# Attention and two MLP layers on one core: the last two blocks of the first layer as one of 512 tokens, 40 masks on ScalarE, tail products in another order

## The chip, the cores and the metric

The kernel runs on one core of a Trainium2 chip. The metric is the device time in microseconds (us) of one execution. The five engines of the core (TensorE, VectorE, ScalarE, GpSimd, SyncE) each take their instructions in the order in which the program lists them; in the rows below they are PE (with PEld for its weight loads), DVE, ACT, POOL and SP. An instruction waits on its engine until what it reads has been written, and everything listed behind it on that engine waits with it.

## The reference

```python
# q, k, v: (4, 8, 576, 64); tau: a scalar; x: 2304 tokens of 512; d_ff: 2048
scores = scale * np.matmul(q, k.transpose(0, 1, 3, 2))
thresh = np.max(scores, axis=-1, keepdims=True) - tau
scores = np.where(scores >= thresh, scores, -1000000000.0)
attn = np.exp(scores - np.max(scores, axis=-1, keepdims=True))
attn = attn / (np.sum(attn, axis=-1, keepdims=True) + 1e-09)
x = ...matmul(attn, v), heads joined...           # (2304, 512)
h = x @ w_in; x = np.maximum(h, 0.0) ** 2 @ w_out            # first layer
h = x @ w_in2; out = h * np.tanh(log1p(exp(h))) @ w_out2     # second layer
```

The weights come as 64-bit floats; the kernel takes them apart with integer operations.

## The kernel before

**Order.** Each piece of work is recorded by `op(opts, fn, r, w, x, due)` or `dma(...)`: the engines that may do it with a planned duration each, the buffers that it reads and writes, and a due time. `Plan.order` then goes forwards and backwards over the recorded pieces, gives each an engine and a place, and emits them in that order. The numbers in `PAR` (due times of the blocks in `blk`, offsets, biases, how many spare buffers each purpose gets) and the planned durations only set that order. So nearly every instruction can change its place when a few of them change.

**Attention.** A pair of heads (`Pair`, 16 of them, 4 per batch entry) has four units of 128 query rows for two heads and one tail unit of the last 64 rows, in which the two heads lie side by side in the 128 partitions. A unit makes scores on PE (`scores`), scales them and takes their row extreme on DVE (`top`, L882), makes the threshold (`most`, L892), takes the exponential on ACT (L908), and on DVE sets what lies under the threshold to zero and sums the row (`mask`, L919). That is 9 masks a pair and 144 in all. Pairs of kind "d" (batch entry 0, and one pair of entry 1) work in float32: PE turns the weights (`turn`, L991), and `turned` or, for the tail, `values` in `values_direct` multiplies with V. The other pairs split the weights into two 16-bit parts, which a DMA turns (`pt`), and `values` in `head` multiplies.

**Tails.** In a tail unit each head has its own 64 columns of the PE array: `pt` is the stationary operand, and the slice `sl` says which half of the columns. Before the change all products of the first head come before those of the second. In `turned` (full units of kind "d") the two heads alternate.

**First layer.** 9 blocks of 256 tokens (`first`, `first_part`); a block's eight parts each make two 128-wide pieces of the hidden layer from x (`mlp_in`, 12 matmuls of 256 columns each, into PSUM buffer `h`), relu and square them on ACT, split them into `gh` and `gl`, and multiply down (`down`, 12 matmuls of 256 columns a piece, into `acc`). A float32 product takes three passes, since both operands are split. Block n needs the attention of all heads for its tokens; block 8 holds the tails of all four entries. Blocks start while attention still runs, and PE takes turns between the two.

**Second layer.** Pairs of blocks as 512 tokens, all its matmuls 512 columns wide (`second`). Its weights (`layer2`) take the places of the first layer's as these come free, and are taken apart by ACT and DVE (`size` L525, `rest` L537, `clamp` L532, `shift` L549, `sign` L555, `to_hi` L583, `to_lo` L594).

**Start.** PE turns the first k and q (`job_direct`, L806), ACT copies them out (L817), then come the first scores. `consts` makes the identity, loads tau and derives from it the scale that `top` uses (L455 to L460). Matmuls of `ones` (`spin`) stand in gaps.

Of the kernel before, what the change touches and what calls it, by code (L numbers as in the profile page):

```python
# [29 lines left out]
    warm=(1, 3, 7),  # L30
    won=("S", "S"),
    land=2.419,
    lag=0.518,
    turns=("h", "s1"),
    kv=(("nat0", "V1"), ("f1", "nat1"), ("KT1", "f0"), ("V0", "KT0")),
    cd=(-150.532, 10.911, -114.568),
    urg=-5.54,
    rawt=23.548,
    kinds="dddd",
    cgen=1.383,  # L40
    split=(),
    ex=dict(cw=1, cr=6, raw=17, pd=2, sc=3),
    exo=("cw", "pd", "sc", "cr", "raw"),
    blk=list((17.026, 77.25, 181.004, 262.558, 368.796, 471.734, 577.967, 790.694, 936.347)),
    tb2=145.883,
    down2=89.229,
    sp=(0, 0),
    off=(170.46, 68.826, 37.695, -205.928, 58.656, 43.101, -191.105, -38.461),
    ahead=(10.872, 128.518, 9.367, -61.853, 3.491, 155.716, -16.749, 483.826, 162.488, -31.72),
    start=-197.714,  # L50
    area=dict(sc=("x0", "x1"), hl=("x2",)),
    jobahead=19.381,
    fbi=6,
    stay=1.0,
    stayt=150.0,
    kinds2="ssss",
    kb=("dhss", "ssss", "ssss"),
)
# [22 lines left out]
class Plan:  # L81
# [6 lines left out]
    BIAS = {"V": 1.26, "A": 0.34, "P": 3.463, "S": 0.46}  # L88
# [239 lines left out]
def attention_moe_moe_kernel(ctx: ExitStack, tc: tile.TileContext, q, k, v, tau, w1i, w1o, w2i, w2o, out):  # L328
# [75 lines left out]
    def rot(*places):  # L404
# [59 lines left out]

# [160 lines left out]
    def pow2(name, raws, junk, due):  # L625
# [24 lines left out]
        op({"T": 0.22}, lambda e: mm(t()[:, 0:n], ones, mx(), True, True), r=[mx, K], w=[t], due=due + 0.1)  # L650
# [123 lines left out]
    def job_direct(p, due):  # L774
# [10 lines left out]
        for x, dst, z, (j0, j1) in todo:  # L785
# [24 lines left out]
            t = op({"T": 0.15 * (j1 - j0)}, turn, r=[raw, K], w=[o], due=due - z)  # L810
# [34 lines left out]
    def unit(p, g, hh, j, due):  # L845
# [24 lines left out]
        op({"T": (1.2 if direct else 0.85) if hh < 2 else 0.65 if direct else 0.48}, scores, r=[QT, KT], w=ss, due=due,  # L870
# [34 lines left out]
    def weigh(p, hh, j, i, sc, m, nt, due):  # L905
        ex = sbuf(place("e", "e0", "e1"), [128, 576], F32)
        op({"A": 0.67},
           lambda e: nc.scalar.activation(  # L908
               out=ex(), in_=sc(), func=AF.Exp, bias=m()[:, i:i + 1], scale=-1.0),
           r=[sc, m], w=[ex], due=due + 1.5 - URG, tab=("exp", "ln"))  # L910
# [5 lines left out]
        l = p.l  # L916

# [10 lines left out]
    def head(p, g, hh, u, ex, due):  # L928
# [35 lines left out]
        op({"T": 0.41 if hh < 2 else 0.9}, values, r=[pt, V], w=[o], due=due + 7 + O_VA, half=1)  # L964
# [3 lines left out]
    def values_direct(p, g, hh, u, ex, last, o, due):  # L968
# [24 lines left out]
        op({"T": 0.6}, turn, r=[ex, K], w=ts, due=due + 2.5 + O_DIR)  # L993
# [38 lines left out]
        op({"T": 1.6}, values, r=[pt, V], w=[o], due=due + 7 + O_VA)  # L1032
        normal(p, g, hh, due)

    def turned(p, j, due):
# [21 lines left out]
        op({"T": 0.14}, lambda e: nc.tensor.transpose(o()[:, 128 * j:128 * j + 128], xt(), ident), r=[xt, K], w=[o], due=due + 1)  # L1057
# [52 lines left out]
    def attention(b, groups, t0, t1, tails):  # L1110
        n = NPR * (4 * len(groups) + tails)
        i = 0
        for pr in range(NPR):
# [4 lines left out]
            p.keep = None  # L1118
# [57 lines left out]
    def x_first(n, due):  # L1176
        xh, xo = sbuf("xh", [128, 2, 4, 128], F32R), sbuf("xo", [128, 2, 4, 128], F32R)
        o = pbuf(rot("s0", "s1"), [128, 1024])
        for t in range(2):
            for g in range(2):  # L1180
# [8 lines left out]
                op({"T": 0.218}, turn, r=[xl, K], w=[o], due=due - 0.5)  # L1189
# [84 lines left out]

    def second():
# [220 lines left out]
```

## Time and profile before

| | |
|---|---|
| median of 3 runs | 1029.93 us (1028.37 to 1031.53) |
| the profiled execution | 1031.52 us, its span 1029.7 us |
| PE busy | 1002.4 us (97%), 8581 matmuls |
| DVE busy | 617.9 us (60%) |
| ACT busy | 622.0 us (60%) |
| PE's share of the chain that ended last | 83% |

The span runs from the first to the last instruction of the profiled execution; its own time is 1.8 us longer. Matmuls overlap in the records, so the time that one costs is read from start to start, not from its own duration.

### The profile page before, as it was taken

What the parts mean: (1) busy time and instruction counts of PE and PEld (TensorE: products, weight loads), DVE (VectorE), ACT (ScalarE), POOL (GpSimd) and SP (SyncE); (2) the same over time, 40 slices, a digit from 0 to 9 for tenths busy, and PEclk for the clock granted to TensorE, in tenths of its full rate; (3) what the DMA queues carried; (4) which work ended last, traced back from release to release, by engine and by line L of the source; (5) the groups of instructions that cost most, each with busy time, mean ns of one, the idle gap of its engine ahead of it and who ended that gap; (6) DMA issues with size and microseconds to landing.
All of it is one profiled execution on the core that took longest, in us unless ns stands there. A gap on an engine that the chain in (4) does not pass through costs nothing.

```text
span 1029.7 us, 21534 instructions
## 1 busy us (share of the span) xinstructions
PE 1002.4 (97%) x8581; PEld 888.2 (86%) x8581; DVE 617.9 (60%) x1442; ACT 622.0 (60%) x1143; POOL 0.8 (0%) x7
## 2 busy tenths in 40 slices
PE   5999999999999999999999999999999999999997
PEld 4666789889888998889999999988888888888897
DVE  5999999998899887989765137971211211211111
ACT  5989999777787877877576459962322332232231
POOL 0000000000000000000000000000000000000000
PEclk9999999999999999999999999999999999999999
DMA  9732247798788988887674123521100110010010
GB/s 286 207 112 86 87 139 146 156 157 174 164 164 150 163 158 172 149 156 137 138 204 149 42 68 108 196 91 30 45 8 1 41 41 1 21 41 1 1 41 21
DMA packets 231188, 109.48 MB, mean 106 GB/s; under 512 B 194608, under 2 KB 212016, under 8 KB 231088
## 3 DMA queue, kind: packets, MB, share of 16 engines
q1 hardware_dynamic: 230816, 107.98, 44.8%
q8 instruction: 67, 1.10, 0.4%
q14 instruction: 33, 0.27, 0.1%
q10 hardware_dynamic: 272, 0.13, 0.0%
HBM read 58.16 MB, written 14.16 MB: 70 GB/s over the span
## 4 chain that ended last, share of the span: by engine, by line
PE 83%; ACT 5%; DMA 5%; DVE 4%; SPq 2%; issue 1%; ACTq 0%; DVEq 0%
PE acc L435 26%; PE s L435 22%; PE h L435 21%; PE small L435 10%; DMA pt<-hl 2%; DMA area<-in_moe_w_in_dram 2%; ACT e L908 1%; SPq L792 1%; DMA f<-in_q_dram 1%; DMA area<-in_moe_w_out_dram 1%; DVE e L919 1%; PE s L1187 1%; PE h L991 0%; PE acc L991 0%; ACT stg L525 0%
## 5 line engine op out<-in xcount | busy, mean ns | idle before, releaser
L435 PE MATMUL acc<-gh,wo 128*128 128x256 f32 x1152 | 215.4, 280 | 0.0
L435 PE MATMUL h<-xh,wi 128*128 128x256 f32 x1152 | 213.2, 279 | 0.8 <-ACT r L1232 0.5
L435 PEld LDWEIGHTS h<-xh,wi 128*128 128x128 f32 x1152 | 182.4, 192 | 4.7 <-issue 1.6
L435 PEld LDWEIGHTS acc<-gh,wo 128*128 128x128 f32 x1152 | 183.0, 192 | 3.8 <-issue 3.0
L435 PE MATMUL h<-xo,wi 128*128 128x256 f32 x576 | 158.4, 275 | 0.0
L435 PE MATMUL acc<-gl,wo 128*128 128x256 f32 x576 | 158.4, 275 | 0.0
L594 DVE TENSOR_TENSOR gl<-r,gh 128x512 fp32r<-128x512 f32 x90 | 62.2, 691 | 157.7 <-ACT gh L583 157.4
L435 PEld LDWEIGHTS acc<-gl,wo 128*128 128x128 f32 x576 | 110.5, 192 | 0.0
L435 PEld LDWEIGHTS h<-xo,wi 128*128 128x128 f32 x576 | 110.5, 192 | 0.0
L435 PE MATMUL s<-KT,area 64*128 64x512 f16 (+7 forms) x840 | 88.3, 333 | 3.9 <-ACT area L817 2.5
L583 ACT ACTIVATE gh<-r 128x512 fp32r<-128x512 f32 x87 | 54.7, 628 | 46.3 <-PE small L435 24.0
L919 DVE SCALAR_TENSOR_TENSOR e<-area,n,e 128x576 f32<-128x576 f32 x93 | 74.9, 815 | 8.9 <-ACT e L908 8.8
L435 PE MATMUL acc<-wo,gh 128*128 128x512 f32 x240 | 79.7, 379 | 0.0
L882 DVE TENSOR_SCALAR_CACHE_REDUCE area<-s,c 128x576 f32<-128x576 f32 x90 | 71.7, 814 | 7.2 <-PE s L435 6.8
L594 DVE TENSOR_TENSOR pt<-area,pt 128x512 fp32r<-128x512 f32 x18 | 12.5, 692 | 102.1 <-ACT pt L583 102.1
L908 ACT ACTIVATE e<-area,m 128x576 f32<-128x576 f32 x93 | 70.0, 765 | 2.7 <-DVE area L948 1.6
L948 DVE TENSOR_TENSOR hl<-e,hl 128x512 f16<-128x512 f32 (+1 forms) x136 | 61.0, 454 | 7.3 <-ACT hl L943 7.2
L1232 ACT ACTIVATE r<-h 128x512 f32<-128x512 f32 x71 | 42.0, 592 | 35.5 <-PE h L435 28.6
L435 PE MATMUL small<-V,pt 128*128 128x64 f16 (+1 forms) x1540 | 58.9, 194 | 2.4 <-DMA pt<-hl 1.7
L435 PEld LDWEIGHTS <-pt 128*128 128x128 f16 (+1 forms) x1540 | 50.4, 101 | 10.1 <-issue 5.9
L943 ACT ACTIVATE hl<-e 128x576 f16<-128x576 f32 x68 | 46.0, 678 | 19.8 <-DVE e L919 10.3
L1282 ACT ACTIVATE r<-s 128x512 f32<-128x512 f32 x17 | 10.2, 601 | 68.4 <-PE s L435 68.4
(306 smaller groups left out, 2050.3 us busy)
## 6 DMA issues: line engine op xcount, KB each, us to landing
area<-in_moe_w_out_dram SPq DMA_DIRECT2D x20, 512.0 KB, 4.1
area<-in_moe_w_in_dram SPq DMA_DIRECT2D x17, 512.0 KB, 3.6
wi<-in_moe_w_in_dram SPq DMA_DIRECT2D x10, 512.0 KB, 4.1
xx<-xdr SPq DMA_DIRECT2D x36, 128.0 KB, 2.6
x2dr<-stg SPq DMA_DIRECT2D x18, 256.0 KB, 3.1
xdr<-xx SPq DMA_DIRECT2D x32, 128.0 KB, 2.2
f<-in_q_dram SPq DMA_DIRECT2D x24, 128.0 KB, 3.1
V<-in_moe_w_out_dram SPq DMA_DIRECT2D x6, 512.0 KB, 4.1
```

What stands on the lines that cost most here:

```text
L435: nc.tensor.matmul(o, l, r, start=start, stop=stop, skip_group_check=True)
L583: nc.scalar.activation(out=o, in_=i, func=AF.Copy)
L594: VEC[e].tensor_tensor(out=part(lo), in0=src(), in1=f32(part(hi)), op=ALU.subtract)
L792: e.dma_start(out=raw()[:, j0:main, h, :], in_=x[h, 0:512, :].rearrange("(p j) d -> p j d", j=4)[:, j0:main, :],)
L882: nc.vector.tensor_scalar(out=sc(), in0=s()[:, 0:576], scalar1=c()[:, 3:4], scalar2=None, op0=ALU.mult, op1=ALU.min, accum_out=m()[:, i:i ...
L908: lambda e: nc.scalar.activation(out=ex(), in_=sc(), func=AF.Exp, bias=m()[:, i:i + 1], scale=-1.0),
L919: nc.vector.scalar_tensor_tensor(out=ex(), in0=sc(), scalar=nt()[:, i:i + 1], in1=ex(), op0=ALU.is_le, op1=ALU.mult, accum_out=l()[:, 0, u ...
L943: nc.scalar.activation(out=hl()[:, 0:576], in_=ex(), func=AF.Copy)
L948: VEC[e].tensor_tensor(out=hl()[:, a:a + n], in0=ex()[:, z:z + n], in1=hl()[:, z:z + n], op=ALU.subtract)
L1187: nc.tensor.transpose(o()[:, z + c:z + c + 128], xl()[:, c:c + 128], ident)
L1232: nc.scalar.activation(out=halves(r()), in_=turned_out(ph()), func=AF.Relu)
L1282: nc.scalar.activation(out=out, in_=in_, func=AF.Mish)
```

## The change

- The last two blocks of the first layer (7 and 8) become one of 512 tokens (`last_two`, `two_part`), with matmuls of 512 columns, two PSUM buffers (`s0`, `s1`) for the hidden pieces, and `acc`, `h` and `small` for the sums.
- In both `values` functions of the tails the two heads alternate.
- 40 of the 144 masks go to ACT: `cut` (an activation with a very steep negative side sends what lies under the threshold to minus infinity) and `exp`, which also sums the row, take the place of the exponential on ACT and the mask on DVE. `pm` gives the number per pair for each batch entry: 16, 12, 4 and 8 in all.
- tau has a load and an operation of its own; identity is made apart from it.
- Turns of kind "d" use `h` alone once `acc` is taken. The buffers of the second layer's weights and x are laid out anew. All numbers of `PAR` that set the order are new.

```diff
-    warm=(1, 3, 7),
+    warm=(1, 3, 6),
-    turns=("h", "s1"),
+    turns=("h",),
+    pm=(4, 3, 1, 2),
...
     def consts(e):
-        make_identity(nc, ident)
-        nc.sync.dma_start(out=tt[:, 3:4], in_=tau.to_broadcast([128, 1]))
...
+        nc.vector.tensor_scalar(out=tt[:, 5:6], in0=tt[:, 1:2], scalar1=-1.0, scalar2=None, op0=ALU.mult)
...
-    op({"S": 0.5}, consts, w=[K], due=-50.0, load=(0.0, 0.7, 0.7))
+    dma(lambda e: e.dma_start(out=tt[:, 3:4], in_=tau.to_broadcast([128, 1])), "tau", w=[KT_], due=-40.0)
+    op({"V": 0.45}, consts, r=[KT_], w=[K], due=-39.0)
...
+        p.n += 1
+        if p.n * PAR["pm"][p.b] % 9 < PAR["pm"][p.b]:
+            def cut(e):
+                nc.scalar.activation(
+                    out=ex(), in_=sc(), func=AF.Prelu, bias=nt()[:, i:i + 1], scale=-1.0, alpha=3e38)
+
+            def exp(e):
+                nc.scalar.activation(
+                    out=ex(), in_=ex(), func=AF.Exp, bias=tt[:, 5:6], accum_out=l()[:, 0, u:u + 1])
...
         def values(e):
-            for h in ((hh,) if hh < 2 else (0, 1)):
-                sl = slice(0, 128) if hh < 2 else slice(64 * h, 64 * h + 64)
-                for i in range(9):
-                    t = 5 * h + (i if i < 5 else i - 5)
-                    mm(o()[sl, 64 * u:64 * u + 64], pt()[:, i, sl], V()[:, t, 0:64], i == 0, i == 8)
-                    if i < 5:
-                        mm(o()[sl, 64 * u:64 * u + 64], pt()[:, i, sl], V()[:, t, 64:128], False, False)
+            for i in range(9):
+                for z in range(0, 128 if i < 5 else 64, 64):
+                    for h in ((hh,) if hh < 2 else (0, 1)):
+                        sl = slice(0, 128) if hh < 2 else slice(64 * h, 64 * h + 64)
+                        t = 5 * h + i % 5
+                        mm(o()[sl, 64 * u:64 * u + 64], pt()[:, i, sl], V()[:, t, z:z + 64],
+                           i == 0 and z == 0, i == 8)
...
         def values(e):
-            for h in (0, 1):
-                sl = slice(64 * h, 64 * h + 64)
-                for i in range(5):
-                    d = slice(0, 128) if i < 4 else slice(64, 128)
+            for i in range(5):
+                d = slice(0, 128) if i < 4 else slice(64, 128)
+                for h in (0, 1):
+                    sl = slice(64 * h, 64 * h + 64)
                     mm(o()[sl, 64 * u:64 * u + 64], pt()[d, i, sl], V()[d, 5 * h + i, :], i == 0, i == 4)
...
+    def two_part(j, x, acc):
+        d = due_p(j)
+        ph = quarter(False)
+        for f in range(2):
+            mlp_in(0, j, f, ph[f], 0, x, d + 0.1 * f, 512)
+        for f in range(2):
...
+            def down(e, j=j, f=f, wo=wo, gh=gh, gl=gl):
+                for dt in range(4):
+                    o = acc[0]()[:, 512 * dt:512 * dt + 512] if dt < 2 else acc[dt - 1]()[:, 0:512]
+                    for i, (l, z) in enumerate(passes(wo, (gh, gl))):
+                        mm(o, l()[:, f, 128 * dt:128 * dt + 128], z().rearrange("p a n b -> p n b a"),
+                           j == 0 and f == 0 and i == 0, j == 7 and f == 1 and i == 2)
...
     def layer2(j):
-        raws = ("raw0", "raw1", "V")
...
+        raws = ("raw0", "raw1", "raw2")
+        order = 8 * "nat0 nat1 pt0 pt1".split()
...
-    for n in range(NB):
+    for n in range(NB - 2):
         at(blk[n], first, n)
+    at(blk[NB - 2], last_two)
```

What this does to the order is shown at three places. The first is SP's queue at the start of the program, where the loads are issued; before:

```order
L500 DMA xh<-in_moe_w_out_dram 128x1024
L792 DMA wo_74<-in_k_dram 128x4x64 x2
L797 DMA wo_74<-in_k_dram 64x2x64
L492 DMA area<-in_moe_w_in_dram 128x2x512
L453 DMA tt<-in_tau_dram 128x1
L792 DMA wo_74<-in_q_dram 128x4x64 x2
L797 DMA wo_74<-in_q_dram 64x2x64
```

and with the change:

```order
L794 DMA wo_75<-in_k_dram 128x4x64 x2
L799 DMA wo_75<-in_k_dram 64x2x64
L794 DMA wi_82<-in_q_dram 128x4x64 x2
L799 DMA wi_82<-in_q_dram 64x2x64
L502 DMA xh<-in_moe_w_out_dram 128x1024
L464 DMA tt<-in_tau_dram 128x1
L502 DMA xo<-in_moe_w_out_dram 128x1024
```

The three loads of k and the three of q now stand first; the first weights (`xh`) went from ahead of them to behind them, and tau from fifth to eighth issue.

The second is ACT's queue at the start; before, up to the first exponentials:

```order
L525 ACTIVATE wo_92<-xh 128x512
L537 ACTIVATE xh<-xh 128x512
L525 ACTIVATE stg<-area 128x512
L583 ACTIVATE wo_112<-wo_92 128x512
L537 ACTIVATE area<-area 128x512
L817 ACTIVATE KT<-s_114 128x576
L583 ACTIVATE wi_136<-stg 128x512
L525 ACTIVATE stg<-area 128x512
L817 ACTIVATE area<-s_127 128x576
```

and with the change, up to the first `cut` (L918) and `exp` (L922):

```order
L819 ACTIVATE KT<-s_91 128x576
L527 ACTIVATE wi_118<-xh 128x512
L819 ACTIVATE area<-s_105 128x576
L539 ACTIVATE xh<-xh 128x512
L527 ACTIVATE wi_118<-xo 128x512
...
L929 ACTIVATE e<-wi_150,m_151 128x576
L918 ACTIVATE e<-wi_150,n_161 128x576
L527 ACTIVATE stg<-area 128x512
L922 ACTIVATE e,l_186<-e,tt 128x576
```

The copies of the turned k and q (L817, now L819) moved from sixth and ninth place to first and third.

The third is PE where blocks 7 and 8 begin; a part of block 8 before (x in `xh` and `xo`; each row one or two matmuls):

```order
L435 MATMUL h<-xh,wi_565 128x256
L435 MATMUL h<-xo,wi_565 128x256
L435 MATMUL h<-xh,wi_565 128x256 x2
L435 MATMUL h<-xo,wi_565 128x256
...
L435 MATMUL acc<-gh_9302,wo_112 128x256
L435 MATMUL acc<-gl_9318,wo_112 128x256
```

and the first part of the joined block (x in `KT`, `V`, `f`, `e`), behind block 6's last products:

```order
L437 MATMUL acc<-gl_8716,wo_2135 128x256
L437 MATMUL acc<-gh_8714,wo_2135 128x256
L437 MATMUL s_8768<-KT,wi_274 128x512
L437 MATMUL s_8768<-V,wi_274 128x512
L437 MATMUL s_8768<-KT,wi_274 128x512 x2
L437 MATMUL s_8768<-V,wi_274 128x512
L437 MATMUL s_8768<-KT,wi_274 128x512
```

The same number of tokens now takes half as many matmuls, each of twice the columns: 384 of 512 for 768 of 256.

## Rows read from the trace of the kernel before

**Rows 1.** Busy time by stage: us, then each engine (instructions), PEclk, DMA share, GB/s.
```profile
0.00:16.00 16.00, 6.33 (x22) 4.58 (x24) 5.66 (x13) 7.40 (x12) 0.84 (x7) 1.00 0.89 278
16.00:120.00 104.00, 96.73 (x831) 68.75 (x828) 100.64 (x259) 93.01 (x198) 0.00 (x0) 0.98 0.49 142
120.00:530.00 410.00, 405.30 (x4839) 365.45 (x4839) 358.09 (x933) 317.77 (x591) 0.00 (x0) 1.00 0.79 156
530.00:656.00 126.00, 125.46 (x1086) 124.03 (x1085) 70.26 (x114) 87.07 (x147) 0.00 (x0) 1.00 0.33 109
```

**Rows 2.** PE's timeline, 640 to 656 us: start, duration, what, [idle before].
```profile
641.27 0.28 PE L435 MATMUL h<-xo,wi 128*128 128x256 f32 x1
...
643.61 0.28 PE L435 MATMUL h<-xo,wi 128*128 128x256 f32 x1
...
653.22 0.38 PE L435 MATMUL s<-f,wi 128*128 128x512 f32 x1
...
655.81 0.38 PE L435 MATMUL s<-f,wi 128*128 128x512 f32 x1
```

**Rows 3.** All 16-bit tail products as one group: xcount, busy, mean ns, idle before.
```profile
L435 PE MATMUL small<-V,pt 128*64 128x64 f16 x308 | 10.7, 197 | 1.6 <-DMA pt<-hl 1.3 <-DVE xx L1067 0.3
```

**Rows 4.** PE's timeline around one 16-bit tail.
```profile
295.43 0.97 PE L435 MATMUL small<-V,pt 128*64 128x64 f16 x28
296.33 0.38 PE L435 MATMUL h<-xh,wi 128*128 128x256 f32 x1
```

**Rows 5.** PE's timeline around one float32 tail.
```profile
48.21 1.80 PE L435 MATMUL small<-V,wo 128*64 128x64 f32 x20
49.94 0.66 PE L991 MATMUL h<-ident,e 128*128 128x128 f32 x4
```

**Rows 6.** PE's timeline in `turned`, whose two heads (`wo`, `wi`) alternate.
```profile
27.24 0.32 PE L435 MATMUL small<-wo,V 128*64 128x128 f32 x1
27.24 0.32 PE L435 MATMUL small<-wi,V 128*64 128x128 f32 x1
27.40 0.27 PE L435 MATMUL small<-wo,V 128*64 128x128 f32 x1
```

**Rows 7.** PE's timeline at the start.
```profile
5.70 1.38 PE L806 MATMUL s<-ident,wo 128*128 128x128 f32 x5 [3.91 <-DMA wo<-in_k_dram]
9.37 1.39 PE L806 MATMUL s<-ident,wo 128*128 128x128 f32 x5 [2.29 <-DMA wo<-in_q_dram]
...
15.24 2.40 PE L435 MATMUL s<-KT,area 64*128 64x512 f32 x8 [2.48 <-ACT area L817]
```

**Rows 8.** SP's timeline at the start: issues.
```profile
0.74 0.40 SPq L500 DMA_DIRECT2D xh<-in_moe_w_out_dram  x1
...
2.60 0.64 SPq L797 DMA_DIRECT2D wo<-in_k_dram  x1
...
3.92 0.47 SPq L453 DMA_DIRECT2D tt<-in_tau_dram  x1
...
5.70 0.63 SPq L797 DMA_DIRECT2D wo<-in_q_dram  x1
```

**Rows 9.** ACT's and DVE's timelines at the start.
```profile
4.38 0.66 ACT L525 ACTIVATE wo<-xh 128x512 f32<-128x512 f32 x1 [2.36 <-DMA xh<-in_moe_w_out_dram]
...
8.51 0.15 DVE L455 TENSOR_SCALAR tt<-tt 128x1 f32<-128x1 f32 x1 [8.51 <-DMA tt<-in_tau_dram]
...
17.67 0.82 DVE L882 TENSOR_SCALAR_CACHE_REDUCE wi<-s,cd 128x576 f32<-128x576 f32 x1 [0.27 <-PE s L435]
```

**Rows 10.** DVE up to block 0's x: its first low part, and busy times till then.
```profile
119.27 0.69 DVE L1204 TENSOR_TENSOR xo<-s,xh 128x512 fp32r<-128x512 f32 x1
...
8.50:119.30 110.80, 100.18 (x836) 71.36 (x837) 105.59 (x270) 97.04 (x205) 0.00 (x0) 0.98 0.53 157
```

**Rows 11.** Mask and exponential as groups: busy, mean ns, idle before.
```profile
L919 DVE SCALAR_TENSOR_TENSOR e<-area,n,e 128x576 f32<-128x576 f32 x93 | 74.9, 815 | 8.9 <-ACT e L908 8.8
L908 ACT ACTIVATE e<-area,m 128x576 f32<-128x576 f32 x93 | 70.0, 765 | 2.7 <-DVE area L948 1.6 <-DVE hl L948 0.6 <-DVE l L936 0.2
```

More of the change, by code (lines that the diff above doesn't have):

```diff
@@ L29 @@
     merge=8,
-    warm=(1, 3, 7),
+    warm=(1, 3, 6),
     won=("S", "S"),
-    land=2.419,
-    lag=0.518,
-    turns=("h", "s1"),
+    land=1.932,
+    lag=0.832,
+    turns=("h",),
     kv=(("nat0", "V1"), ("f1", "nat1"), ("KT1", "f0"), ("V0", "KT0")),
-    cd=(-150.532, 10.911, -114.568),
-    urg=-5.54,
-    rawt=23.548,
+    cd=(-160.029, 12.621, -161.281),
+    urg=-15.443,
+    rawt=22.691,
     kinds="dddd",
-    cgen=1.383,
+    cgen=7.952,
     split=(),
[L42 to L46, printed above, removed]
+    ex=dict(cw=4, cr=2, raw=32, pd=2, sc=5),
+    exo=("cr", "cw", "sc", "pd", "raw"),
+    blk=list((25.72, 84.953, 185.792, 266.428, 370.172, 474.28, 578.7, 808.575, 941.026)),
+    tb2=136.032,
+    down2=92.619,
     sp=(0, 0),
-    off=(170.46, 68.826, 37.695, -205.928, 58.656, 43.101, -191.105, -38.461),
-    ahead=(10.872, 128.518, 9.367, -61.853, 3.491, 155.716, -16.749, 483.826, 162.488, -31.72),
-    start=-197.714,
+    off=(192.543, 61.874, 12.17, -239.53, 56.556, 58.809, -204.681, -78.195),
+    ahead=(21.758, 102.326, 4.716, -50.865, 1.704, 145.102, -26.751, 495.329, 152.712, 63.594),
+    start=-183.005,
     area=dict(sc=("x0", "x1"), hl=("x2",)),
-    jobahead=19.381,
+    jobahead=19.847,
     fbi=6,
-    stay=1.0,
-    stayt=150.0,
+    stay=1.5,
+    stayt=220.0,
     kinds2="ssss",
     kb=("dhss", "ssss", "ssss"),
+    pm=(4, 3, 1, 2),
 )
@@ L906, in weigh @@
         ex = sbuf(place("e", "e0", "e1"), [128, 576], F32)
[L907 to L910, printed above, removed]
         u = 2 * hh + j if hh < 2 else 0
@@ L916, in weigh @@
         l = p.l
+        p.n += 1
[6 more added lines that the diff above has]
+                    out=ex(), in_=ex(), func=AF.Exp, bias=tt[:, 5:6], accum_out=l()[:, 0, u:u + 1])
+            op({"A": 0.67}, cut, r=[sc, nt], w=[ex], due=due + 1.5 - URG, tab=("exp", "ln"))
+            op({"A": 0.76}, exp, r=[K], x=[ex], w=[l], due=due + 1.9 - URG, tab=("exp", "ln"))
+            return u, ex
+        op({"A": 0.67},
+           lambda e: nc.scalar.activation(
+               out=ex(), in_=sc(), func=AF.Exp, bias=m()[:, i:i + 1], scale=-1.0),
+           r=[sc, m], w=[ex], due=due + 1.5 - URG, tab=("exp", "ln"))
         def mask(e):
@@ L1273, in first_part, with xtile, __init__, __call__ @@
                     "x2", r=[st], w=[x2_dr[n][h]], due=due_f(n, 7) + 7)
+    def xtile(z):
+        return plan.buf(
+            z, lambda: sb.tile([128, 2, 2, 2, 128], F32R, name=z, tag=z), over=HALF[z][3] if z in HALF else ()
+        )
+    class Columns:
+        def __init__(self, bufs, k):
+            self.bufs, self.k = bufs, k
+        def __call__(self, c):
+            return self.bufs[c // 2]()[:, 0:self.k, :, c % 2, :].rearrange("p n a b -> p n b a")
+    def due_p(j):
+        return blk[7] + (blk[9] - blk[7]) * j / 8.0
@@ new lines, in last_two, with turn, src, hi @@
+    def last_two():
+        due = due_p(0)
+        hs, os_ = (xtile("KT"), xtile("f")), (xtile("V"), xtile("e"))
+        for t, n in enumerate((7, 8)):
+            assert len(x_dr[n].wr) == (NPR if n < 8 else NPR * B)
+            o = pbuf(rot("s0", "s1"), [128, 1024])
+            for g in range(2):
+                for a in range(2):
+                    xl = sbuf(rot("xl0", "xl1"), [128, 256], F32)
+                    dma(lambda e, xl=xl, n=n, a=a, g=g: e.dma_start(
+                        out=xl(), in_=x_dr[n]()[:, a, 256 * g:256 * g + 256]),
+                        "xl", r=[x_dr[n]], w=[xl], due=due - 4)
+                    def turn(e, o=o, xl=xl, z=512 * a + 256 * g):
+                        for c in (0, 128):
+                            nc.tensor.transpose(o()[:, z + c:z + c + 128], xl()[:, c:c + 128], ident)
+                    op({"T": 0.218}, turn, r=[xl, KI], w=[o], due=due - 0.5)
+                def src(o=o, g=g):
+                    return o().rearrange("p (a c b) -> p a c b", a=2, c=4)[:, :, 2 * g:2 * g + 2, :]
+                def hi(e, src=src, t=t, y=hs[g]):
+                    if e == "A":
+                        nc.scalar.activation(out=y()[:, t], in_=src(), func=AF.Copy)
+                    else:
+                        nc.vector.tensor_copy(out=y()[:, t], in_=src())
+                def lo(e, src=src, t=t, y=hs[g], z=os_[g]):
+                    nc.vector.tensor_tensor(out=z()[:, t], in0=src(), in1=f32(y()[:, t]), op=ALU.subtract)
+                op({"A": 0.52, "V": 0.6}, hi, r=[o], w=[hs[g]], due=due - 0.4 - URG)
+                op({"V": 0.6}, lo, r=[o, hs[g]], w=[os_[g]], due=due - 0.3 - URG)
+        x = Columns(hs, 2), Columns(os_, 2)
+        acc = [pbuf("acc", [128, 1024]), pbuf("h", [128, 512]), plan.buf("o0", lambda: small, over=("o1", "o2"))]
+        for j in range(NJ):
+            at(due_p(j), two_part, j, x, acc)
```

89 lines of the change are left out of this document (60 added, 29 removed).

## The prediction, made blind

> **What bounds the kernel now.** I read the busy times by stage first [rows 1]. PE is busy for 405.3 of 410 us between 120 and 530 us and for 125.5 of 126 in the stage behind; until 16 us it lacks 9.7 us, from 16 to 120 us another 7.3. So from 120 us on the time is the sum of what PE streams, and a microsecond taken from PE there is a microsecond off the end, unless a new wait takes its place. Ahead of 120 us it is another matter: from 8.5 us to block 0's x, DVE is busy for 105.6 of 110.8 us [rows 10], so there DVE sets the pace as much as PE does.
>
> Then I read PE's timeline from start to start, since the durations overlap: what one matmul costs is the distance to the next.
>
> **The sum, part by part.** It is made against the profiled execution (1031.5 us, span 1029.7); the median of the runs shown is 1.6 us lower, and the predicted time is the median less the gain.
>
> *Blocks 7 and 8 as one of 512 tokens.* From 641.27 to 643.61 us PE starts 21 matmuls of 256 columns (three in each 0.33 us): 2.34 / 21 = 0.1114 us each. From 653.22 to 655.81 it starts 12 of 512 columns: 2.59 / 12 = 0.2158 us each [rows 2]. Two blocks have 8 parts x 2 pieces x 24 products x 2 = 768 matmuls of 256, which become 384 of 512. Each pair saves 2 x 0.1114 - 0.2158 = 0.0070 us, so 384 x 0.0070 = 2.7 us. Both figures are measured on the same kind of product, so the bounds are narrow, 2 to 3 us.
>
> The Trainium skill ("TensorE: Matmul & The Clock Gate", Back-to-back issue gap) gives the warm distance between isolated matmuls as N / 2.4 GHz and 2.5 ns more. By it a pair would save 2 x 109.2 - 215.8 = 2.6 ns, an estimate of 1.0 us for the 384, and the predicted time would be 1020.0 us. The row at 512 columns agrees with it (215.8 ns), the one at 256 does not (111.4 ns); the rows decide.
>
> *16-bit tails.* 308 products [rows 3] are 11 tails of 28. One takes 296.33 - 295.43 = 0.90 us [rows 4]. No row shows these with the heads in turn. The nearest is `turned`, which does alternate, with the same column halves: both heads' products start at 27.24, the next pair 0.16 us later [rows 6]. There the second head lies wholly beside the first. So the price is bounded by 0.90 (nothing overlaps) and 0.45 (all does); I take 0.50, near the row, since 14 pairs each have two weight loads and so little streaming to hide them. 11 x 0.40 = 4.4 us, bounds 0 and 5.0. All eleven lie where PE is the bound.
>
> *Float32 tails.* There are five (kind "d" four times in entry 0, once in entry 1). One takes 49.94 - 48.21 = 1.73 us [rows 5]; by the same row of `turned`, between 0.87 and 1.73. I take 0.98, so 0.75 saved. Three of the five lie ahead of block 0, where DVE is late anyway; I count two, 1.5 us (bounds 0 and 4.3 for all five).
>
> *The start.* k's last load is issued at 2.60 us and PE begins to turn it at 5.70, 3.1 us later; q's at 5.70, turned from 9.37, 3.7 us later [rows 7, 8]. In the new order SP issues k's three loads first and q's right behind. An issue takes some 0.67 us with the gap behind it [rows 8], so the last of k starts at 0.74 + 1.4 = 2.1 and the last of q at 4.1 us; PE turns k at 5.2 and q at 7.8 to 9.2 us. Before, ACT's copy of q came only after weights' work that waits for DVE, so the first scores start at 15.24, 4.5 us after q was turned. Now the copy has two operations ahead of it: k's copy, and the first weights, whose load is issued at 4.8 us and so lands at 8.4 (3.64 us, as from 0.74 to 4.38 [rows 8, 9]). The copy runs from 9.2 to 9.9 us, and scores start at 9.9: 5.3 us sooner. tau is issued at 5.2 instead of 3.92 and lands 4.6 us later as before [rows 8, 9], at 9.8, in time for the first reduction on DVE at about 12.3 (17.67 before).
>
> How much of the 5.3 us lasts depends on DVE. Between 8.5 and 119.3 us it was idle for 5.2 us (110.8 less 105.6 [rows 10]). It now begins 1.3 us later (9.8), and although 16 masks leave it in that stretch, the order gives it other pieces for them (9 copies, 7 shifts, one more pair of score reductions): counted by kind and priced at the distances of the trace, it has some 3 us less to do than before up to block 0's x. With that idle time kept, block 0's x comes 3.1 - 1.3 = 1.8 us sooner, with one more unit of scores done by then, which is worth one or two more. I take 3 us; bounds 0 (DVE and ACT give it all back) and 5.3 (all lasts).
>
> *40 masks on ACT.* DVE loses 40 x 0.815 = 32.6 us, ACT gains 40 x 0.765 = 30.6 at least [rows 11]; `cut` and the sum in `exp` are not in this trace, and the exponential over the same 128x576 is the nearest row. From 120 us on both are off the path (DVE 358 and ACT 318 of 410 us [rows 1]), so I price this at nothing. Its cover is that slack; if it is gone, PE waits for turned weights. In the stretch before 120 us ACT has 93 of 104 us and gets some 5 more, which I have charged to the start.
>
> *Second layer's places and the rest.* Its weights used to be taken apart during block 8 and on into the second layer, PE busy throughout that stage [rows 1]; the joined block gives them twice as long from its first part on. No term. PE's waits after 120 us (4.7 us) may shift either way: 0, bounds -3 and +3.
>
> Sum: 2.7 + 4.4 + 1.5 + 3 = 11.6 us. Profiled execution 1019.9; median 1029.9 - 11.6 = **1018.3 us**.
>
> **The rivals.**
>
> *A, the start is given back.* DVE and ACT together have no less to do before block 0, ACT begins its weights 4 us later than at 4.38 [rows 9], and each ACT mask is two instructions in a row on an engine that also copies for PE. For it: DVE's 95% before 119.3 us [rows 10]. Against: first scores are 5.3 us sooner on paper and both engines have idle time. Then only 2.7 + 4.4 + 1.5 = 8.6 us are left: 1021.3 us, or 1022.8 if the float32 tails go with it.
>
> *B, alternating heads gain nothing.* The products are 64 columns wide, not 128 as in `turned`, so weight loads may set the pace, and these may not overlap. Then 2.7 + 3 = 5.7 us: 1024.2 us. Rows 6 speak against it.
>
> The Trainium skill (the same page, Part 3: Packing small matmuls) says that weight loads overlap running matmuls only where the row groups differ; here both heads use the same 128 rows and differ in columns alone. By it the tails keep their price and the time is B's. No row here shows the loads themselves; that two heads start together on the same rows [rows 6] is against it.
>
> *C, slower: the joined block waits for its hidden pieces.* By the order, a part's pieces are used 10.4 us after they are made (one part down and one part up between them, 4 x 2.6 us), and ACT and DVE work them off between the weights of the second layer, in one queue. If a weight operation stands there and waits for its load or its place, each part is late by what is past that cover, eight times. The change then only turns slower past (11.6 + 3.1) / 8 = 1.8 us per part; at 2.5 us it is 1018.3 + 20 = 1038.3 us. Against: from 530 to 656 us the same kinds of work took ACT 87 of 126 us and PE lacked 0.5 [rows 1].
>
> *D, it shows nothing:* A and B together, 2.7 us or 1027.2, which is within what a measurement tells (0.3%, 3.1 us).
>
> **How the numbers follow.** My forecast has 0.55 (its own range 1013 to 1021, from bounds of tails and start), a larger gain (all upper bounds, 2.7 + 5.0 + 4.3 + 5.3 + 3 = 20.3, so down to 1009.6) 0.05, A 0.18, B 0.07, D 0.06, C 0.09. Below 1012 I leave out 0.05, above 1026 D and C, 0.15: range 1012 to 1026. Faster by over 0.3% (below 1026.8): forecast, larger gain, A and B, 0.85. Same 0.06. Slower 0.09, all C and its like.
>
> **What would show it.** First scores at 9.9 us (within 1). 384 matmuls of 512 columns 0.2158 us apart where blocks 7 and 8 were, without a wait of PE. A 16-bit tail of 28 products in 0.50 us, a float32 one in 1.0. Block 0's x about 2 us sooner than 119.3. DVE's busy time lower by 15 to 33 us, ACT's higher by 10 to 30. Waits of PE between 16 and 120 us of 7 to 10 us; over 10 is A. The prediction is wrong if tails keep 0.90 us (B), if PE's waits behind 530 us exceed 3 us (C), or if waits between 120 and 530 us grow past 8 us, which would mean that ACT has become late there.

## The result, and the profile after

The changed kernel takes 1017.88 us (median of 4 runs, 1016.92 to 1018.24), the kernel before 1029.15 us in the same runs: ratio 0.9885, 95% interval 0.9866 to 0.9905. That is 11.3 us less, against 11.6 forecast (1018.3). Timed once more, beside some of the experiments, the ratio was 0.9886 (0.9869 to 0.9902).

Busy times by stage of the changed kernel, as in [rows 1]:

```profile
0.00:16.00 16.00, 10.10 (x40) 7.16 (x41) 4.15 (x13) 6.84 (x11) 0.85 (x7) 0.86 0.72 200
16.00:120.00 104.00, 95.39 (x847) 67.13 (x847) 99.56 (x261) 98.52 (x218) 0.00 (x0) 0.96 0.55 159
120.00:530.00 410.00, 404.13 (x4866) 365.97 (x4865) 344.86 (x888) 328.49 (x626) 0.00 (x0) 1.00 0.80 153
530.00:656.00 126.00, 126.00 (x714) 113.25 (x713) 93.97 (x149) 105.93 (x172) 0.00 (x0) 1.00 0.46 154
```

PE lacks 8.6 us of 104 in the second stage, 5.9 of 410 in the third and nothing in the fourth, where the joined block stands. DVE is busy for 601.0 us in all (617.9 before), ACT for 636.7 (622.0): DVE loses 16.9 us and ACT gains 14.7, about half of what the forecast counted for the masks.

PE's timeline, the places of [rows 7, 5, 4, 2] in turn: start, one float32 tail, one 16-bit tail, one part of the joined block.

```profile
4.39 1.38 PE L808 MATMUL s<-ident,wo 128*128 128x128 f32 x5 [2.09 <-DMA wo<-in_k_dram]
...
6.73 1.38 PE L808 MATMUL s<-ident,wi 128*128 128x128 f32 x5
...
11.72 2.40 PE L437 MATMUL s<-KT,area 64*128 64x512 f32 x8 [2.30 <-ACT area L819]
...
70.31 0.95 PE L437 MATMUL small<-V,wo 128*64 128x64 f32 x20
71.19 0.66 PE L808 MATMUL s<-ident,wi 128*128 128x128 f32 x4
...
193.23 0.63 PE L437 MATMUL small<-V,pt 128*64 128x64 f16 x28
193.79 0.38 PE L437 MATMUL h<-xh,wi 128*128 128x256 f32 x1
...
590.89 0.38 PE L437 MATMUL s<-KT,wi 128*128 128x512 f32 x1
...
596.07 0.38 PE L437 MATMUL acc<-gh,wo 128*128 128x512 f32 x1
```

A float32 tail takes 71.19 - 70.31 = 0.88 us (1.73 before), a 16-bit one 0.56 (0.90 before). Between the last two rows 24 matmuls start, 5.18 / 24 = 0.2158 us each, without a wait.

ACT's and DVE's timelines at the start, and DVE's first low part of block 0's x, as in [rows 9, 10]:

```profile
10.48 0.66 ACT L527 ACTIVATE wi<-xh 128x512 f32<-128x512 f32 x1 [4.02 <-DMA xh<-in_moe_w_out_dram]
11.04 0.64 ACT L819 ACTIVATE area<-s 128x576 f32<-128x576 f32 x1
...
10.89 0.15 DVE L455 TENSOR_SCALAR tt<-tt 128x1 f32<-128x1 f32 x1 [10.89 <-DMA tt<-in_tau_dram]
...
14.25 0.81 DVE L884 TENSOR_SCALAR_CACHE_REDUCE wi<-s,cd 128x576 f32<-128x576 f32 x1
...
117.27 0.69 DVE L1219 TENSOR_TENSOR xo<-s,xh 128x512 fp32r<-128x512 f32 x1
```

ACT stood before the first weights' load until 10.48 us, with q's copy queued behind; so the first scores came at 11.72, not at the 9.9 of the forecast. SP had issued that load at 4.81 us, as forecast, but it took 5.7 us to land, where the prediction had 3.64. Block 0's x comes 2.0 us sooner than in [rows 10].

### The profile page after: what moved, and what is told of

Same layout as the page of the kernel before. It is cut to its first block, busy times and chain, and to the rows that moved or that the text cites. A ratio compares the mean times of both kernels' runs of the same rounds, so it can differ in the third digit from the quotient of the medians.

```text
span 1016.5 us, 20689 instructions
## 1 busy us (share of the span) xinstructions
PE 991.2 (98%) x8195; PEld 866.9 (85%) x8195; DVE 601.0 (59%) x1395; ACT 636.7 (63%) x1194; POOL 0.9 (0%) x7
## 4 chain that ended last, share of the span: by engine, by line
PE 74%; ACT 6%; DVE 4%; DMA 3%; issue 2%; SPq 1%; ACTq 0%; DVEq 0%
PE s L437 24%; PE acc L437 23%; PE h L437 16%; PE small L437 9%; DMA pt<-hl 1%; DMA f<-in_q_dram 1%; ACT e L929 1%; DVE e L934 1%; SPq L716 1%; ACT e L922 1%; PE s L1202 1%; DVE area L884 1%; ACT e L918 1%; DVE hl L963 1%; DMA pt<-area 0%
## 5 line engine op out<-in xcount | busy, mean ns | idle before, releaser
L437 PE MATMUL acc<-gh,wo 128*128 128x256 f32 (+1 forms) x960 | 190.1, 287 | 0.0
L437 PE MATMUL h<-xh,wi 128*128 128x256 f32 x912 | 169.9, 280 | 0.6 <-ACT r L1247 0.5
L437 PEld LDWEIGHTS acc<-gh,wo 128*128 128x128 f32 x960 | 154.7, 192 | 4.5 <-issue 2.5
L437 PEld LDWEIGHTS h<-xh,wi 128*128 128x128 f32 x912 | 144.7, 192 | 4.0 <-issue 1.9
L437 PE MATMUL acc<-gl,wo 128*128 128x256 f32 (+1 forms) x480 | 135.4, 282 | 0.0
L437 PE MATMUL h<-xo,wi 128*128 128x256 f32 x456 | 125.4, 275 | 0.0
L437 PEld LDWEIGHTS acc<-gl,wo 128*128 128x128 f32 x480 | 92.0, 192 | 1.1 <-DVE gl L596 0.2
L437 PEld LDWEIGHTS h<-xo,wi 128*128 128x128 f32 x456 | 87.5, 192 | 0.0
L437 PE MATMUL s<-KT,wi 128*128 128x512 f32 x192 | 64.9, 379 | 0.0
L437 PE MATMUL s<-f,wi 128*128 128x512 f32 x192 | 64.9, 379 | 0.0
```

The source lines that it names most:

```text
L437: nc.tensor.matmul(o, l, r, start=start, stop=stop, skip_group_check=True)
```

## The experiments

Each kernel was timed beside the kernel before; "by the ratio" is the difference of two ratios times 1029 us. One ratio's interval is 1.2 to 2.0 us to either side, and a difference of two has some 2.4, so differences under that are not settled by the times alone. Where two kernels have the same order, the traces tell more: I matched DVE's instructions one to one and took the difference of their starts. Medians of this difference, in us (positive is later), by the place in us in the kernel that stands second in each row:

| | 20-30 | 40-60 | 100-120 | 160-200 | 300-350 | 450-500 | 900-1000 |
|---|---|---|---|---|---|---|---|
| float32 tails back - changed | -0.1 | -1.0 | 1.1 | 2.1 | 2.1 | 1.7 | 2.2 |
| 16-bit tails back - changed | -0.2 | -0.4 | -0.3 | -0.3 | 1.2 | 2.1 | 2.8 |
| 512 split - changed | -0.5 | -1.5 | -1.5 | -1.5 | -1.8 | -2.5 | 0.8 |
| tails alone - before | -0.9 | -1.5 | -2.3 | -2.9 | -5.3 | -7.1 | -6.5 |
| 40 masks back - changed | -0.6 | 3.6 | 10.6 | 12.8 | 14.4 | 15.5 | 15.6 |
| 24 masks back - changed | 0.1 | -0.5 | -0.4 | 2.1 | 4.5 | 5.3 | 5.5 |
| masks alone - before | -0.1 | 1.1 | 5.4 | 6.7 | 8.2 | 7.9 | 7.5 |
| copy sooner - changed | -0.5 | -1.3 | -1.3 | -1.4 | -3.0 | -2.6 | -2.4 |
| loads sooner - changed | -0.9 | -0.4 | -0.4 | -0.3 | -2.0 | -2.6 | -2.6 |
| other beginning - changed | -1.7 | -3.6 | -3.6 | -3.6 | -4.0 | -4.4 | -4.4 |
| the same, products ahead - changed | -0.7 | -1.1 | -1.1 | -1.1 | -1.4 | -1.4 | -0.9 |
| changed, again - changed | -0.5 | -0.9 | -0.9 | -0.9 | -1.2 | -1.5 | -1.1 |

The last row is scatter: two executions of one kernel differ by 0.9 us after the start, where the first ran longer at half clock (last section), and by 0.2 more in the end. So only growth behind 40 us is read off the first rows.

**Float32 tails back.**

```diff
-            for i in range(5):
-                d = slice(0, 128) if i < 4 else slice(64, 128)
-                for h in (0, 1):
-                    sl = slice(64 * h, 64 * h + 64)
+            for h in (0, 1):
+                sl = slice(64 * h, 64 * h + 64)
+                for i in range(5):
+                    d = slice(0, 128) if i < 4 else slice(64, 128)
```

> The changed kernel with only the five float32 tails' products back in the old order (one head after the other); everything else, the order on all engines too, as changed. In the changed kernel such a tail takes 0.878 us, before 1.728, so 0.85 is in question, five times. Theory 1 (PE's own time is the path also ahead of block 0, all five tails count): 4.2 us slower than the changed kernel. Theory 2 (the step on record: DVE is late anyway ahead of block 0, so only two of the five count): 1.7 us slower, with the rest gone from PE's waits between 16 and 120 us. Rival B (alternating heads gain nothing): 0.

Ratio 0.9914 (0.9902 to 0.9927): 3.0 us slower. The difference grows from -1.0 to 2.1, by 3.1 us, in steps of 0.6, 0.9, 0.7 and 0.9 behind the tails at 48, 70, 91 and 120 us; the fifth, at 153 us, shows no step of its own. So the three ahead of block 0's x count as well: theory 1, less what the waits take up.

DVE's waits from 40 to 120 us show why DVE doesn't hide them (engine, tile and line <- what it waited for: us, times, longest). The two longest in the changed kernel:

```profile
DVE xx L1082 <- ACT e L929: 0.9, 1, 0.9
DVE e L934 <- ACT e L929: 0.7, 1, 0.7
```

And with the tails back:

```profile
DVE e L934 <- ACT e L929: 1.6, 2, 0.9
DVE xx L1082 <- ACT e L929: 1.3, 1, 1.3
```

In all, DVE waits 2.0 us longer for ACT there and ACT 1.6 us longer for PE, while PE's own waits of 0.3 us and more are the same. So in this order DVE is late because PE is. Block 0's x moves with the tails:

```profile
118.41 0.68 DVE L1219 TENSOR_TENSOR xo<-s,xh 128x512 fp32r<-128x512 f32 x1
```

That is 1.1 us later than in the changed kernel's first trace and 2.1 later than in its second (116.33), whose stretch at half clock is as long as here.

**16-bit tails back.** The same edit in `values` of `head`.

> The changed kernel with only the eleven 16-bit tails' products back in the old order (one head after the other). Such a tail takes 0.562 us in the changed kernel and 0.901 before. If each microsecond of PE counts where they lie: 11 x 0.339 = 3.7 us slower than the changed kernel. The step on record had 0.50 us, 4.4 in all. Rival B: 0.

Ratio 0.9918 (0.9905 to 0.9931): 3.4 us slower. The difference grows by 3.1 us from 160 us on (-0.3 to 2.8). So most of PE's own 11 x 0.34 = 3.7 us counts.

**512 columns split into two of 256.**

```diff
-                        mm(o, l()[:, f, 128 * dt:128 * dt + 128], z().rearrange("p a n b -> p n b a"),
-                           j == 0 and f == 0 and i == 0, j == 7 and f == 1 and i == 2)
+                        for g in (0, 1):
+                            mm(o[:, 256 * g:256 * g + 256], l()[:, f, 128 * dt:128 * dt + 128],
+                               z().rearrange("p a n b -> p n b a")[:, g],
+                               j == 0 and f == 0 and i == 0 and g == 0, j == 7 and f == 1 and i == 2 and g == 1)
```

> The changed kernel with each matmul of 512 columns of the joined block issued as two of 256 behind each other, with the same weights; places, order and all else as changed. If the width alone is the gain, by the step on record (0.1114 against 0.2158): 2.7 us slower than the changed kernel, with 768 starts some 0.1114 us apart. If the joined block's gain is what the sums from start to start in the two traces show for its kind of work, 4.5 us: 4.5 slower. If two with the same weights need only N / 2.4 GHz and 2.5 ns each: 1.0 us.

The hidden pieces' matmuls (`mlp_in`) are split in the same way. Ratio 0.9907 (0.9894 to 0.992): 2.3 us slower, not settled by the times. In the trace the difference is -2.1 at 530 us and 0.8 from 700 us on: 2.9 us, against the 2.7 of the record. PE's timeline in the split part; 16 matmuls start between the two rows:

```profile
600.77 0.39 PE L437 MATMUL s<-KT,wi 128*128 128x256 f32 x2
...
602.56 0.61 PE L437 MATMUL s<-f,wi 128*128 128x256 f32 x4
```

1.79 / 16 = 0.112 us each, though here two in a row have the same weights. The Trainium skill ("TensorE: Matmul & The Clock Gate", Back-to-back issue gap) would have, by its formula for isolated matmuls, 0.109 here and 1.0 us in all; the runs give 2.9.

**Tails alone, in the kernel before.** Both edits turned round, all else as before.

> The kernel before with only the two kinds of tails alternating between the heads, all else and the order as before. Put back into the old order in the changed kernel they cost 2.7 us (float32) and 3.2 us (16-bit) by the medians. If they are worth the same in the kernel before: 5.9 us faster than before, about 1023.3 us. By the step on record (4.4 + 1.5): 5.9 too, but with 16-bit tails of 0.50 us; by PE's own time alone 8.0. Rival B: 0.

Ratio 0.9950 (0.9938 to 0.9962): 5.1 us faster. The 16-bit tails bring 3.6 us again (-2.9 to -6.5). The float32 ones bring only 1.4 (-1.5 to -2.9), 1.1 of it from 100 us on. (The -1.5 stands there ahead of the first tail; it goes with the clock, which in the kernel before fell to 0.91 and 0.66 in the two windows from 20 to 28 us and here was full.) One edit, two orders: 1.4 us in the old, 3.1 in the new.

**40 masks back to DVE.**

```diff
-                    out=ex(), in_=sc(), func=AF.Prelu, bias=nt()[:, i:i + 1], scale=-1.0, alpha=3e38)
+                    out=ex(), in_=sc(), func=AF.Exp, bias=m()[:, i:i + 1], scale=-1.0)
...
-                nc.scalar.activation(
-                    out=ex(), in_=ex(), func=AF.Exp, bias=tt[:, 5:6], accum_out=l()[:, 0, u:u + 1])
+                nc.vector.scalar_tensor_tensor(
+                    out=ex(), in0=sc(), scalar=nt()[:, i:i + 1], in1=ex(), op0=ALU.is_le, op1=ALU.mult,
+                    accum_out=l()[:, 0, u:u + 1],
+                )
```

> The changed kernel with the 40 masks back on DVE: ACT's first operation is the plain exponential, and the mask with its sum stands on DVE where ACT's second stood in the order (two of them one place earlier); all else, the order on PE too, as changed. Theory 1 (up to block 0's x DVE sets the pace, there 16 of the masks are 13 us; behind it they cost nothing): DVE is busy for 99.6 of 104 us between 16 and 120 us, so 13 us less the 4.4 that it idles come late there, 5 to 10 us slower in the end, PE's waits between 16 and 120 us up by as much, and none after 120 us. Theory 2 (the place of the masks moves nothing, as in the term of nothing on record): 0 to 1 us. Theory 3 (two instructions in a row on ACT delay it): up to 3 us faster.

Ratio 1.0036 (1.0022 to 1.005): 15.5 us slower than the changed kernel, slower even than the kernel before, and over the top of every theory. Busy times of two stages:

```profile
16.00:120.00 104.00, 89.79 (x755) 62.16 (x754) 100.05 (x265) 78.13 (x163) 0.00 (x0) 0.93 0.54 148
120.00:530.00 410.00, 398.94 (x4789) 357.88 (x4789) 359.73 (x938) 311.06 (x582) 0.00 (x0) 1.00 0.79 148
```

DVE is as full as before up to 120 us (100.05), so the 16 masks, 13 us, can only make it late, while ACT falls from 98.5 to 78.1. But 4 us more arise between 120 and 350 us, where DVE idles for 50 of 410.

**24 masks back, those behind entry 0.** The same edit, only where `p.b` is over 0.

> The changed kernel with 24 of the 40 masks back on DVE, those of the entries 1 to 3 of the batch; the 16 of entry 0, which lie ahead of 120 us, stay on ACT; order as changed. With all 40 on DVE the same step of DVE's work came 11.4 us later at 120 us, 14.7 us later at 200 to 250 us and 15.6 at the end. Theory 1 (the term of nothing on record holds where DVE has slack, and the 4 us behind 120 us were the late stage before it): 0 to 1 us slower than the changed kernel. Theory 2 (masks on DVE delay PE behind 120 us too): 3 to 5 us slower, the delay arising between 120 and 250 us.

Ratio 0.9944 (0.9930 to 0.9957): 6.1 us slower; in the trace 4.9 us arise from 110 to 350 us. Theory 2, by the ratio somewhat over its 5 us. Busy times, and PE's waits from 120 to 350 us (as above):

```profile
120.00:530.00 410.00, 399.72 (x4799) 361.09 (x4798) 356.80 (x927) 310.16 (x577) 0.00 (x0) 1.00 0.78 149
```

```profile
PE small L437 <- DVE xx L1092: 2.6, 3, 0.9
PE small L437 <- DMA pt<-hl: 2.2, 3, 1.6
PE small L437 <- ACT xt L1105: 1.2, 2, 0.9
PE s L1212 <- ACT xh L1224: 0.7, 1, 0.7
PE s L437 <- DVE area L884: 0.6, 2, 0.4
...
```

The same view of the changed kernel:

```profile
PE small L437 <- DVE xx L1082: 1.6, 3, 0.7
PE small L437 <- DMA pt<-hl: 1.4, 1, 1.4
PE s L1202 <- ACT xh L1214: 0.7, 1, 0.7
PE h L1006 <- ACT e L922: 0.3, 1, 0.3
```

DVE idles 53 of 410 us, and PE is still busy for 4.4 us less than in the changed kernel. PE waits longer for what stands behind the masks: the normalized output (`xx`, `xt`: 2.2 us more) and the weights that the DMA turns (`pt`: 0.8 more, but that wait differs by 0.7 between two executions of the changed kernel too). My reading, not tested mask by mask: a place in the order that was made for a mask on ACT has no room for 0.8 us on DVE, however much room there is on average.

**Masks alone, in the kernel before.** The reverse: there the same 40 (of 144; the 143 below is a slip) go to ACT, `cut` in the exponential's place (behind the threshold's), `exp` in the mask's.

> The kernel before with only 40 of its 143 masks moved to ACT (the same share of each pair's as in the changed kernel: 16 in entry 0): cut where the exponential stood, exponential with the sum where DVE's mask stood; PE's order and all else as before. In the changed kernel's order the move back to DVE cost 15.8 us. Theory 1 (the move frees DVE, which sets the pace ahead of block 0's x, in any order): 3 to 7 us faster than before, since PE waits 7.3 us between 16 and 120 us and 4.7 until 530. Theory 2 (the masks pay only in an order that gives DVE other pieces for them; in the old order ACT, with 93 of 104 us busy and 12 more to do, becomes late instead): 0 to 8 us slower than before. Theory 3 (the term of nothing on record): within 1 us of before.

Ratio 1.0084 (1.0069 to 1.0099): 8.6 us slower than before. Theory 2, just over its range. Busy times and PE's longest wait, 16 to 120 us:

```profile
16.00:120.00 104.00, 93.17 (x788) 65.34 (x786) 85.02 (x212) 98.89 (x219) 0.00 (x0) 1.00 0.48 134
```

```profile
PE small L1074 <- ACT pt L1069: 4.5, 4, 1.4
```

DVE falls from 100.6 to 85.0 us and gains nothing by it; ACT rises from 93.0 to 98.9 and is late with the copies for PE (that wait is 2.2 us before). So the masks have no price of their own: moved by themselves they lose in either direction.

**q's copy ahead of the first weights on ACT.** The numbers in this edit and the next are those of recorded pieces: 456 is the first weights' operation on ACT, 19 the copy of q, 455 and 2 the loads of the first weights and of tau.

```diff
+    seq.remove(456)
+    seq.insert(seq.index(19) + 1, 456)
```

> The changed kernel with ACT's first piece of weights, which waits for its load until 10.48 us, moved behind the copy of q, for which PE waits 2.3 us until 11.72 us. First scores at some 8.8 to 9.1 us in place of 11.72. Theory 1 (PE's time is the path from the start on): 2 to 2.9 us faster than the changed kernel, as the step on record wanted from the start. Theory 2 (DVE sets the pace ahead of block 0, and it waits for tau until 10.9 us): DVE's operations at 30 us no more than 0.5 us earlier, and 0 to 0.7 us at the end.

Ratio 0.9879 (0.9863 to 0.9894), 0.6 us faster, not settled by the time. First scores came at 9.87 us in place of 11.72, but DVE's first reduction at 13.87 in place of 14.25: it stands behind tau (10.96 us) and four operations on weights. At the start theory 2 holds. Behind 40 us another 1.1 us arise, from 200 to 350 us, and they fit one wait of PE: for a DMA's turn (`pt<-hl`) it waits 1.4 us once in the changed kernel between 160 and 530 us, 0.7 in its second execution, and not at all here. That this wait is gone because of the edit isn't shown.

**First weights and tau loaded ahead of k and q.**

```diff
+    for n in (2, 455):
+        seq.remove(n)
+        seq.insert(0, n)
```

> The changed kernel with the first weights' load and tau's issued ahead of those of k and q on SP's queue. Both land some 5 us sooner, k and q 1.3 to 2 us later; first scores between 9.7 and 11 us, DVE's first operations on tau at 6 us in place of 10.9. Theory 1 (PE's time is the path): 0.7 to 2 us faster, as much as the first scores come sooner. Theory 2 (DVE's beginning is the path): 2 to 4 us faster, with DVE's operations at 30 us that much earlier. If k's later landing (PE already waits 2.1 us for it) decides: 0 to 1.5 us slower.

Ratio 0.9873 (0.986 to 0.9886), 1.2 us faster, again not settled. DVE had tau at 4.82 us, but ACT worked on the weights only behind k's copy, and the first scores were at 12.19. No theory's mechanism got its chance: 2.2 of the 2.6 us in the table arise behind 160 us, where the wait for the DMA's turn is gone as in the kernel above.

**Another beginning.** This puts the two together: loads as in the last kernel, ACT at once on the weights (457, 456), DVE's third operation on them sooner (460), and four of the `ones` products (13 to 16) behind the first scores.

```diff
+    for n in (2, 455):
+        seq.remove(n)
+        seq.insert(0, n)
+    for n, z in ((457, 10), (456, 457), (460, 466)):
+        seq.remove(n)
+        seq.insert(seq.index(z), n)
+    for n in (16, 15, 14, 13):
+        seq.remove(n)
+        seq.insert(seq.index(21) + 1, n)
```

> The changed kernel with another beginning: loads of the first weights and of tau first, ACT works on these weights ahead of k's and q's copies, four of PE's warming products go behind the first scores, and DVE's third operation on the weights ahead of that on the next ones. DVE can begin at some 5 us and do 1.6 us of the weights before the first scores, which come at some 10.6 us; the second reduction's end, at 19.47 us in the changed kernel, comes at 16.7 to 17.5. Theory 1 (what DVE gains at the start is gained in the end): 2 to 3 us faster than the changed kernel. Theory 2 (the start is given back to later waits or to the half clock of PE, as most of it was in the two runs before): 0 to 1 us.

1014.10 us, ratio 0.9850 (0.9835 to 0.9865): it beats both kernels, the changed one timed beside it (below) by 3.7 us. That is theory 1, over its 2 to 3 us; block 0's x comes at 113.68 us.

**The changed kernel again.**

> The changed kernel once more, on the chip on which the other kernels of this call run, as their yardstick: 1017 to 1018.5 us. Half clock of PE somewhere between 11 and 27 us, at another place than in the first run if its place varies from run to run.

1017.55 us, ratio 0.9886, as expected.

**The other beginning with the four products left ahead of the scores.** Without the last three lines of that edit.

> The kernel with the other beginning (loads of the first weights and tau first, ACT and DVE on these weights before the first scores), but with the four warming products left ahead of the first scores, as in the changed kernel. With them behind the scores the granted clock was full all through and the kernel 3.4 us faster than the changed one. Theory 1 (the gain is the clock, held by those four): half clock again for some us between 11 and 27, first scores at 12.2 us, 2 to 3 us of the gain lost, ratio to the kernel before 0.987 to 0.988. Theory 2 (the gain is DVE's earlier beginning): at most 0.7 us lost, ratio 0.985 to 0.9858.

Ratio 0.9872 (0.9855 to 0.9888): 2.3 us of the gain are lost, as theory 1 has it; the times alone hardly settle it, but the traces have 2.5 us from 35 us on and 3.5 at the end. Busy times (PEclk is the third figure from the end) of the changed kernel again, then the other beginning, then the one with the products ahead:

```profile
16.00:20.00 4.00, 2.41 (x8) 1.48 (x7) 4.00 (x10) 3.89 (x9) 0.00 (x0) 0.60 1.13 317
20.00:24.00 4.00, 4.00 (x21) 3.34 (x17) 3.50 (x10) 1.58 (x3) 0.00 (x0) 0.55 1.21 243
```

```profile
16.00:20.00 4.00, 3.09 (x19) 1.80 (x16) 4.00 (x11) 3.66 (x8) 0.00 (x0) 1.00 1.15 291
20.00:24.00 4.00, 4.00 (x42) 3.06 (x41) 4.00 (x11) 3.52 (x7) 0.00 (x0) 1.00 0.75 170
```

```profile
16.00:20.00 4.00, 2.41 (x12) 1.39 (x12) 4.00 (x9) 3.89 (x9) 0.00 (x0) 1.00 1.15 296
20.00:24.00 4.00, 4.00 (x20) 3.32 (x17) 4.00 (x12) 2.40 (x5) 0.00 (x0) 0.59 1.01 194
```

And one group of PE's timeline, the first turns of the weights, in the other beginning and with the products ahead:

```profile
19.67 0.77 PE L1006 MATMUL acc<-ident,e 128*128 128x128 f32 x5
```

```profile
20.73 1.33 PE L1006 MATMUL acc<-ident,e 128*128 128x128 f32 x5
```

The turns start 1.06 us later, since the scores did; then they run at half clock, 1.33 us in place of 0.77, and from 35 us on the kernel is 2.5 us behind. So of these 2.5 us about 1.1 are the later scores and, as the rest, 1.4 the clock: the size was theory 1's, its cause only about half of it.

## Why the prediction was right, and where its steps were not

- **Joined block, 2.7 us: right.** 2.9 between the traces (2.3 by the ratio, not settled alone), and no wait of PE there. Rival C did not come: from 530 to 656 us PE is busy throughout.
- **16-bit tails, 4.4 us: too large.** The row of `turned` was the right guide, and rival B is out; but a tail takes 0.56 us, not 0.50, so PE's gain is 3.7, of which 3.1 to 3.6 us arrive. The Trainium skill (the same page, Part 3: Packing small matmuls) has weight loads overlap running matmuls only between different row groups. The prediction took from it that the tails would keep their price, since the heads share all 128 rows and differ in columns; a tail went from 0.90 to 0.56 us, so that price was wrong. The loads themselves weren't measured.
- **Float32 tails, 1.5 us: the step that failed.** The size of one was right (0.88 us for 0.98). "Three of the five lie ahead of block 0, where DVE is late anyway; I count two" fits the old order, where all five bring 1.4 us, and is false of the new, where they bring 3.1. I priced them in the trace of before, where DVE's busy share looked like the limit. The share is the same in the new order (99.6 of 104 us against 100.6), but there DVE waits for ACT and ACT for PE when the tails are slow.
- **Start, 3 us: the size fits what is left, the chain doesn't.** The three terms measured come to 2.9 + 3.1 + 3.1 = 9.1 us of 11.3; 2.2 remain for start, masks and new order together (3.1 if the gain and its terms are all taken by the ratio), and the whole gain is itself known to some 2 us only. So the 3 us are not contradicted, and not shown. The first scores were 3.5 us sooner, not 5.3, since the first weights' load landed at 10.5 us, not 8.4, with q's copy behind it on ACT. Block 0's x came 2.0 us sooner, close to the forecast (1.8), but by luck: the 1.8 had no tails in it, and with the float32 tails back x comes at 118.41, only 0.9 us sooner than before (with a longer stretch at half clock ahead of it). PE also runs at half clock for some 14 us of the profiled start (7 in the second execution, 3.4 in the kernel before), which the prediction had not foreseen.
- **Masks, nothing: the figure can't be tested alone, and its reason fell.** "Its cover is that slack" is wrong: 24 masks put back on DVE, in the stage where 13% of DVE is idle, cost 6.1 us. In the change, order and masks were laid out together, and what the masks bring there can't be told apart from the order: how the 2.2 us divide between start, masks and order stays open. The busy times were mis-sized too: with all 40 back DVE is busy for 629.3 us and ACT for 611.6, so the masks are 28.3 us of DVE and 25.1 of ACT (32.6 and at least 30.6 forecast), and the new order gives DVE 10 to 11 us of ACT's other work.
- **Second layer and waits, nothing: right.** PE lacks 5.9 us from 120 to 530 (4.7 before), none to 656.

So the total was right partly because two errors cancelled: 1.3 us too much for one kind of tail, 1.6 too little for the other.

## What to carry to other kernels

Idle time on average covers nothing by itself in a fixed order: ask at which place the moved instruction will stand and who stands behind it, and move work between engines only with a new order. Whether a microsecond of PE counts depends on who waits for whom there in the new kernel, and a busy share of 95% doesn't tell it: price such edits in both cases when the change also alters the order. At a start, bring forward the whole chain (loads, the second engine's first work, PE's first products) at once; one link alone gave at most 1.2 us, unsettled, all together 3.7, of which some 2.3 hang on four products of PE that stood in the way.

## What the runs showed of the hardware

- PE's granted clock falls to half (1.2 GHz) for some us in the first 30 us in 11 of the 14 traces, at no fixed place: in the changed kernel it is half throughout 12 to 24 us in one execution (0.50 in each slice of 4 us, two of them below), in the next one full until 16 and 0.60 and 0.55 behind it. Only the other beginning and the kernels with the old order and one edit show it full from 16 to 28 us. Over whole executions the other beginning was granted 0.999 to 1.0, the same with the four products ahead 0.996 to 0.998, the changed kernel 0.993 to 0.997. Four products moved into a gap of PE were what differed between full and half in that pair: with them ahead of the scores PE idles for 1.59 us of the slice from 16 us on and the clock falls in the next one, with them behind it idles for 0.91 us and the clock stays full. That the longer idle time is the reason isn't shown.

```profile
12.00:16.00 4.00, 4.00 (x14) 2.47 (x15) 3.39 (x8) 3.38 (x7) 0.00 (x0) 0.50 1.12 329
20.00:24.00 4.00, 4.00 (x18) 3.07 (x16) 3.50 (x10) 1.72 (x3) 0.00 (x0) 0.50 1.15 247
```

- Products on different column halves of the array, alternating, overlap although they share all rows: 28 in 0.56 us (0.020 each), 20 float32 records in 0.88 us (0.044 each), against 0.032 and 0.086 each with one head after the other.
